# Layout of the prepared second-layer weights in DRAM, the pair job's places and one product's turn in a three-stage network on one Trainium2 core

## The chip, the core and the metric

The kernel runs on one core of a Trainium2 chip. The metric is the time of one launch in device microseconds (us). Five instruction streams run side by side: TensorE (PE, matmuls; its weight loads are PEld), VectorE (DVE), ScalarE (ACT), GpSimd (POOL) and SyncE (SP). Here SP issues all DMAs; its queue is shown as SPq. Each engine works through its own list in order and waits at semaphores for the others.

## What is computed

Attention with a window and a few global tokens gives 2176 rows of 512. Two networks follow, one a mixture of eight experts, one plain:

```python
x = attn_out.transpose(0, 2, 1, 3).reshape(2176, 512)
P = exp(x @ w_gate - max)                       # then 8 rounds of scaling rows and columns
for e in range(8):                              # w1: 512 x 1024, w2: 1024 x 512 per expert
    out += P[:, e:e+1] * (np.maximum(x @ w1[e], 0) @ w2[e])
h = out @ w_in                                  # 512 x 2048
y = np.where(h > 0, h, np.exp(np.minimum(h, 0)) - 1) @ w_out
```

All is float32. TensorE takes its operands as a rounded high part (names with h) and the remainder as a low part (l), so a product is three matmuls: high by high, high by low and low by high.

## The kernel before

**Products.** The large products are made by the seven-product method for 2 by 2 blocks: sums and differences of blocks of the weights (`t1` to `t4`) and of the activations (`s1` to `s4`) are prepared, seven products are taken, and their results are added up. Blocks that need no sum are called by row and column: `11`, `12`, `21`, `22`. "Prepared weights" are those sums and blocks, each as a high and a low part.

**Stages.** Up to about 240 us: attention and the first units. From 240 to about 860 us, the **first pass**: fourteen units (half an expert each) over the first 1024 tokens, by `mix_0`, layer one on lines L1383 to L1385 into banks `q`, layer two on L158 to L162. Beside its products a unit prepares the weights of the next one and stores them in DRAM, as the second pass needs them again: `pw1` for the expert's layer one (`store1`), `pw2` for its layer two (`weights2`, with `store` for the sums and `store_raw` for the plain blocks). From 860 to about 1600 us, the **second pass**: the other tokens, sixteen units of two halves each (g=0 with 256 columns, g=1 with 320), by `mix_1`; `load2` brings the prepared weights of layer two back. From 1600 us: the **last network**, whose layer one loads its prepared `w_in` from `wq` by `layer_one` (7 names, high and low, 14 loads of 128 KB at each of 14 calls, 196 in all).

**Jobs beside the units.** The weights of the last network are prepared in pieces beside the units. A **pair** (`weights64_pair`) takes two chunks of `w_in`, builds one unit's seven operands and stores them to `wq`; units 2, 4 and 6 of the first pass hold one each, and units 23, 24, 25, 27 and 28 (the second pass begins with 14) the other five. Other jobs are `prepare` (units 15, 17, 19, 21), `back` (16, 18, 20, 22), which turns finished rows over, and in the first pass `xr` sums (units 3, 5, 7, 9), whose loads stand among the next unit's.

**What sets the order.** SP's queue takes DMAs in the order in which the program gives them. In the first pass the steps of a unit go to two lists that `mix_0` works off, `side1` and `side2`. `lds`, the job's loads, stand at the end of `side2`. In the second pass the steps of a job are put at places of a unit given by `SPOTS`; places below 22 lie in g=0, the others in g=1. The products of a half are ordered by `MIX_1`: `a` and `b` are the two chains of layer one (128 columns of the prepared weights each), `t` the products of layer two, `p` and `tx` those left over from before. In that list the number is the product.

**Which banks.** In `Fold`, products 1, 6, 7 and 4 of a chain add up in one bank, `f1` (`BANK`). After products 1, 6 and 7 ScalarE copies the bank out (`s1`, `u2`, `u3`, by `KEEP`, line L1392) and only then may the chain's next product write it. After `a7` VectorE adds `u3` to a stored part (`t`, L798), and ScalarE makes `v22` of it (L1530). After `t1` ScalarE copies its bank to `f2` (L1629), the seed that t6 adds to. The next operand's high part `hs4` is a ScalarE cast (L1543).

**Stores of a pair before** (L1094): for each of high and low part, seven DMAs, each of two pieces of 128 numbers (512 bytes) for a partition.

```python
for i, v in enumerate((t[:, 0], t[:, 1], t[:, 2], p1[:, 256:], p0[:, :256], p1[:, :256], t[:, 3])):
    nc.sync.dma_start(wq[q][:, u, i, :, k], v.rearrange("p (f c) -> p f c", f=2))
```

The raw blocks of `pw2` (L945) go in four DMAs for each part, each of two pieces of 256 numbers (1 KB) for a partition.

Of the kernel before, what the change touches and what calls it, by code (L numbers as in the profile page):

```python
# [11 lines left out]
F32 = mybir.dt.float32  # L12
# [39 lines left out]
    "pair": (4, 6, 7, 9, 10, 12, 13, 15, 17, 19, 20, 21, 22, 23, 25),  # L52
# [8 lines left out]
MIX_1 = "a1 b1 p4 a2 b2 p3 a6 b6 a5 b5 a7 b7 t1 a4 b4 a3 t6 b3 t2 t5 t7 tx"  # L61
# [8 lines left out]
WORDER = ("t1", "t3", "t4", "22", "11", "21", "t2")  # L70
XORDER = ("11", "12", "21", "22", "s1", "s2", "s3", "s4")
XUSE = ("11", "12", "s2", "s1", "s3", "22", "s4")
W2ORDER = ("11", "t2", "21", "22", "t1", "t3", "t4")
# [12 lines left out]
def tile_net(ctx: ExitStack, tc, kq, vw, vc, qg, wg, w1, w2, wi, wo, consts, out):  # L86
    nc = tc.nc
    U1 = 2 * E
    U2 = F2 // FU
# [18 lines left out]
    wq = {p: dram.tile([128, U2, 7, 2, 2, 128], F32, tag="wq" + p, name="wq" + p) for p in "hl"}  # L108
    pw1 = {p: dram.tile([128, U1, 7 * 512], F32, tag="pw1" + p, name="pw1" + p) for p in "hl"}
    pw2 = {p: dram.tile([128, U1, 8, 512], F32, tag="pw2" + p, name="pw2" + p) for p in "hl"}  # L110
# [802 lines left out]

    def weights2(u):
        v = {}
# [21 lines left out]
        def store(n):  # L937
            for q, t in (("h", v[n, "h"].bitcast(F32)), ("l", v[n, "l"])):
                nc.sync.dma_start(pw2[q][:, u, W2ORDER.index(n)], t)

        def store_raw(q):
            for n in ("11", "12", "21", "22"):
                i, j = int(n[0]) - 1, int(n[1]) - 1
                o = pw2[q][:, u, 7 if n == "12" else W2ORDER.index(n)]
                nc.sync.dma_start(  # L945
                    o.rearrange("p (k f) -> p k f", k=2), w2s[q][:, 2 * i:2 * i + 2, 256 * j:256 * j + 256].bitcast(F32)
                )
# [25 lines left out]
    def prepare(second, u):  # L973

        src, dst, order = ((w1, pw1, WORDER), (w2, pw2, W2ORDER + ("12",)))[second]
# [17 lines left out]
        def lo(n):  # L993
            comb(blk(n).bitcast(F32R), blk(n), v[n, "h"].bitcast(F32), ALU.subtract)
            i = order.index(n)
            for q, t in (("h", v[n, "h"].bitcast(F32)), ("l", blk(n))):
                o = dst[q][:, u, i * 512:(i + 1) * 512] if not second else dst[q][:, u, i]
                nc.sync.dma_start(o.rearrange("p (k f) -> p k f", k=2), t)
# [67 lines left out]
    def weights64_pair(u, k):  # L1066
# [24 lines left out]
        def store():  # L1091
            for q, t, p1, p0 in (("h", c1.room(F32, 4), c1.p, c0.p), ("l", c0.room(F32, 4), c1.t, c0.t)):
                for i, v in enumerate((t[:, 0], t[:, 1], t[:, 2], p1[:, 256:], p0[:, :256], p1[:, :256], t[:, 3])):
                    nc.sync.dma_start(wq[q][:, u, i, :, k], v.rearrange("p (f c) -> p f c", f=2))  # L1094
# [71 lines left out]
    def layer_one(u, f, names=WORDER):  # L1166
        for n in names:
            for q in "hl":
                nc.sync.dma_start(
                    wop[n + q][:, :, f * 128:f * 128 + 128].bitcast(F32), wq[q][:, u, WORDER.index(n), f]  # L1170
                )
# [500 lines left out]
    def load2(u, names):  # L1672
        for n in names:
            for q in "hl":
                i = W2ORDER.index(n) if n != "12" else 7
                o = W2ORDER.index(n if n != "12" else "t2")
                nc.sync.dma_start(fold["all" + q][:, o * 512:(o + 1) * 512].bitcast(F32), pw2[q][:, u, i])
# [25 lines left out]
    with tc.manual_schedule():  # L1703
# [89 lines left out]
        for a, u in enumerate(range(2, U1)):  # L1793
# [11 lines left out]
            if build1:  # L1805
                side2.extend(mingle(build2, steps + build1[:8]))
                loads2, casts, build2 = weights2(u + 1)
                side2.extend(loads2 + build1[8:] + lds)
            else:
                side2.extend([lambda: second_x(XUSE, GS[1][0], SL)] + mingle(build2, steps))  # L1810
# [234 lines left out]
```

## Time and profile before

| | us |
|---|---|
| median of 3 runs | 2014.83 (2011.32 to 2018.03) |
| the profiled execution | 2016.9 |
| its span | 2015.1 |
| TensorE busy | 1899.3 (94% of the span) |
| VectorE busy | 1416.9 (70%) |
| ScalarE busy | 987.3 (49%) |
| DMA engines, mean share of the span | 67.6% |

All rows come from the one profiled execution; times are counted from the start of its span. A row of the timeline gives the start, the length, the engine, the line, the operation, what it writes and from what, shapes, and a count where several alike follow one another. A bracket at its end tells how long the engine was idle before it and what it was waiting for. The rows of stretches give, for a window, its length, each engine's busy time with its instructions, the granted clock of TensorE as a share of full speed (1.00 is 2.4 GHz, 0.50 is 1.2 GHz), the busy share of the 16 DMA engines, and the rate. That share can come out a little above 1.00.

### The profile page before, as it was taken

Reading aid. Unit: us, or ns where it says so; the run is one execution under the profiler, and the core shown is the slowest. Engines: PE = TensorE matmul, PEld = TensorE weight load, DVE = VectorE, ACT = ScalarE, POOL = GpSimd, SP = SyncE. Lnnn points to the kernel's source line nnn. Section 1 sums busy time; section 2 is a strip of 40 time slices with the busy share of each in tenths; the row PEclk is TensorE's granted clock in tenths of the full one; section 3 lists DMA queues with packets and bytes.
Section 4 is the critical chain, followed back from the end, with each engine's and each line's share of the span. In section 5 each row is a group of like instructions: output and inputs, shape, how many; then the busy total and the mean of one; then the engine's idle time right before and its main releaser. Section 6 shows DMA issues by size and latency. Waiting matters only on the chain.

```text
span 2015.1 us, 35891 instructions
## 1 busy us (share of the span) xinstructions
PE 1899.3 (94%) x13345; PEld 1677.7 (83%) x13345; DVE 1416.9 (70%) x2783; ACT 987.3 (49%) x2125; POOL 272.5 (14%) x294
## 2 busy tenths in 40 slices
PE   8999999798989999999999999898989999999999
PEld 6877777676767787799999999888988987788998
DVE  4554877575767568657767777777677578888887
ACT  5453443343434334356555555455555554555664
POOL 2135222222222222100000000000000000002322
PEclk9999999898989999999999999999999999999999
DMA  7585776767677767887786878555655796654431
GB/s 248 195 282 173 270 268 236 272 233 278 234 286 293 276 234 284 269 301 267 244 285 235 292 248 288 176 191 201 220 189 184 246 300 193 189 201 155 121 116 68
DMA packets 338638, 465.52 MB, mean 231 GB/s; under 512 B 35104, under 2 KB 212768, under 8 KB 335136
## 3 DMA queue, kind: packets, MB, share of 16 engines
q1 hardware_dynamic: 338464, 463.24, 67.6%
q8 instruction: 105, 1.72, 0.3%
q14 instruction: 69, 0.57, 0.1%
HBM read 282.12 MB, written 181.01 MB: 230 GB/s over the span
## 4 chain that ended last, share of the span: by engine, by line
PE 49%; DVE 14%; DMA 6%; ACT 4%; issue 2%; SPq 2%; POOL 0%; DVEq 0%; ACTq 0%; POOLq 0%
PE m L162 4%; PE f L1383 4%; PE m L160 4%; PE m L158 4%; PE f L1385 4%; PE f L1384 4%; PE f L1621 4%; PE f L1623 4%; PE f L1622 4%; PE q L1322 2%; PE q L1321 2%; PE q L1320 2%; DVE acc L1458 2%; PE q L1383 2%; PE q L1384 2%
## 5 line engine op out<-in xcount | busy, mean ns | idle before, releaser
L162 PE MATMUL m<-w2h,hl 128*128 128x512 f32 x784 | 309.9, 395 | 4.9 <-DVE hl L1284 3.4
L158 PE MATMUL m<-w2h,hh 128*128 128x512 f32 x784 | 309.1, 394 | 5.7 <-DVE aside L1913 3.0
L160 PE MATMUL m<-w2l,hh 128*128 128x512 f32 x784 | 309.4, 395 | 3.1 <-POOL w2l L154 3.1
L1284 POOL TENSOR_TENSOR hl<-eg,hh 128x288 fp32r<-128x288 f32 (+1 forms) x80 | 57.0, 722 | 1114.2 <-DMA xs4h<-xo3h 983.7
L162 PEld LDWEIGHTS m<-w2h,hl 128*128 128x128 f32 x784 | 147.9, 189 | 39.6 <-DVE hl L1284 6.7
L158 PEld LDWEIGHTS m<-w2h,hh 128*128 128x128 f32 x784 | 148.1, 189 | 35.7 <-DVE aside L1913 3.3
L160 PEld LDWEIGHTS m<-w2l,hh 128*128 128x128 f32 x784 | 148.1, 189 | 33.9 <-POOL w2l L154 5.2
L1621 PE MATMUL f<-wfh,hs 128*128 128x256 f32 x512 | 149.2, 291 | 3.1 <-ACT f L1629 3.1
L1623 PE MATMUL f<-wfh,ls 128*128 128x256 f32 x512 | 148.1, 289 | 0.0
L1622 PE MATMUL f<-wfl,hs 128*128 128x256 f32 x512 | 148.1, 289 | 0.0
L1621 PE MATMUL f<-wfh,h 128*128 128x256 f32 x384 | 109.4, 285 | 2.1 <-ACT u L1633 2.1
L1421 ACT ACTIVATE hh<-t 128x512 fp32r<-128x512 f32 x64 | 40.6, 635 | 142.8 <-DVE t L798 142.5
L1622 PE MATMUL f<-wfl,h 128*128 128x256 f32 x384 | 108.8, 283 | 0.2 <-DMA wfl<-pw2l 0.2
L1623 PE MATMUL f<-wfh,l 128*128 128x256 f32 x384 | 108.8, 283 | 0.0
L154 POOL TENSOR_TENSOR w2l<-w2r,w2h 128x512 fp32r<-128x512 f32 x56 | 73.2, 1335 | 256.8 <-ACT w2h L150 190.7
L1458 DVE SCALAR_TENSOR_TENSOR acc<-y,pr,acc 128x512 f32<-128x512 f32 x120 | 84.9, 749 | 30.2 <-ACT y L1650 28.4
L1621 PEld LDWEIGHTS f<-wfh,hs 128*128 128x128 f32 x512 | 101.2, 198 | 4.8 <-ACT f L1629 4.4
L1392 ACT COPY u<-f 128x256 f32<-128x256 f32 (+1 forms) x128 | 50.5, 400 | 106.1 <-PE f L1385 103.9
L1623 PEld LDWEIGHTS f<-wfh,ls 128*128 128x128 f32 x512 | 101.5, 198 | 0.0
L1622 PEld LDWEIGHTS f<-wfl,hs 128*128 128x128 f32 x512 | 101.4, 198 | 0.0
L798 DVE TENSOR_TENSOR t<-f,u 128x256 f32<-128x256 f32 (+1 forms) x128 | 58.2, 455 | 60.1 <-ACT u L1392 39.5
L798 DVE TENSOR_TENSOR t<-q,u 128x512 f32<-128x512 f32 x56 | 38.6, 689 | 83.2 <-PE q L1385 49.5
(405 smaller groups left out, 5743.9 us busy)
## 6 DMA issues: line engine op xcount, KB each, us to landing
wfh<-pw2h SPq DMA_DIRECT2D x128, 256.0 KB, 4.5
wfl<-pw2l SPq DMA_DIRECT2D x128, 256.0 KB, 4.9
wh<-pw1h SPq DMA_DIRECT2D x105, 256.0 KB, 5.3
wl<-pw1l SPq DMA_DIRECT2D x105, 256.0 KB, 5.3
pw1h<-wh SPq DMA_DIRECT2D x13, 1792.0 KB, 11.9
pw1l<-wl SPq DMA_DIRECT2D x13, 1792.0 KB, 15.5
wr<-in_w_dram SPq DMA_DIRECT2D x36, 512.0 KB, 7.6
w2r<-in_w_dram SPq DMA_DIRECT2D x28, 512.0 KB, 5.8
```

Of the source, the lines that this page charges most:

```text
L154: e.tensor_tensor(out=lo, in0=src, in1=hi.bitcast(F32), op=ALU.subtract)
L158: nc.tensor.matmul(ps, ah, bh, start=first, stop=False)
L160: nc.tensor.matmul(ps, ah, bl, start=False, stop=False)
L162: nc.tensor.matmul(ps, al, bh, start=False, stop=last)
L798: nc.vector.tensor_tensor(out=o, in0=a, in1=b, op=op)
L1383: nc.tensor.matmul(ps, wh, xh, start=k == 0 and begin, stop=False, skip_group_check=True)
L1384: nc.tensor.matmul(ps, wh, xl, start=False, stop=False, skip_group_check=True)
L1385: nc.tensor.matmul(ps, wl, xh, start=False, stop=k == 1, skip_group_check=True)
L1458: nc.vector.scalar_tensor_tensor(out=acc, in0=y, scalar=scale, in1=acc, op0=ALU.mult, op1=ALU.add)
L1621: nc.tensor.matmul(ps[:, m], hh, wh, start=begin and m == k == 0, stop=False, skip_group_check=True)
L1622: nc.tensor.matmul(ps[:, m], hh, wl, start=False, stop=False, skip_group_check=True)
L1623: nc.tensor.matmul(ps[:, m], hl, wh, start=False, stop=m == k == 1, skip_group_check=True)
```

## The change

1. `wq` has a layout in which a pair's operands lie behind one another: the pair's store is three DMAs for each part (four operands of 4 KB for a partition, two of 2 KB, one of 1 KB) in place of seven. `layer_one` reads two pieces of 512 bytes for a partition in place of one of 1 KB.
2. `pw2` is split. The sums stay in it; the plain blocks go to `pr2`, whose layout is that of the tile in SBUF, so that `store_raw` is one DMA of 1 MB (8 KB for a partition) in place of four. `load2` reads a plain block as two pieces of 1 KB.
3. In `side2` the job's loads `lds` stand ahead of the last build steps.
4. The places of "pair" are moved back: eight of its steps stay in g=0, where there were twelve; the other seven are in g=1.
5. In `MIX_1` t1 stands between a7 and b7.

```diff
--- before.py
+++ after.py
@@ -49,7 +49,7 @@
 PAIRS = (2, 4, 6, 23, 24, 25, 27, 28)
 SPOTS = {
     "single": (26, 28, 30, 31, 33, 35),
-    "pair": (4, 6, 7, 9, 10, 12, 13, 15, 17, 19, 20, 21, 22, 23, 25),
+    "pair": (8, 10, 12, 13, 15, 16, 18, 20, 22, 24, 27, 29, 31, 33, 34),
     "prepare": (7, 8, 9, 10, 14, 15, 18, 19, 20, 23, 24, 27, 29, 30, 33, 34, 36, 37, 40, 41),
 }
 SEEDED = 6
@@ -58,7 +58,7 @@
 GS = ((0, 256), (256, HALF))
 MIX_0 = "01 05 02 06 11 07 12 04 16 03 15 17"
 MIX_F = "a1 a5 b1 b5 a2 b2 a6 b6 a7 b7 a4 b4 a3 b3"
-MIX_1 = "a1 b1 p4 a2 b2 p3 a6 b6 a5 b5 a7 b7 t1 a4 b4 a3 t6 b3 t2 t5 t7 tx"
+MIX_1 = "a1 b1 p4 a2 b2 p3 a6 b6 a5 b5 a7 t1 b7 a4 b4 a3 t6 b3 t2 t5 t7 tx"
 MIX_L = "a1 b1 p4 a2 b2 p3 a6 b6 a5 b5 a7 b7 t1 a4 b4 a3 b3 t2 t6 t5 t7"
 MIX_E = "p4 t1 p3 t2 t6 t5 t7 t4 t3 tx"
 KEEP = {1: "s1", 6: "u2", 7: "u3"}
@@ -70,6 +70,7 @@
 WORDER = ("t1", "t3", "t4", "22", "11", "21", "t2")
 XORDER = ("11", "12", "21", "22", "s1", "s2", "s3", "s4")
 XUSE = ("11", "12", "s2", "s1", "s3", "22", "s4")
+QORDER = ("t1", "t3", "t4", "t2", "21", "22", "11")
 W2ORDER = ("11", "t2", "21", "22", "t1", "t3", "t4")
 W22 = ("11", "t2", "21", "t3", "t1", "t4", "22")
 TURN_0 = "a1 a6 a2 a7 a5 a4"
@@ -105,9 +106,10 @@
     sf = {p: dram.tile([128, 4, 2, SL], F32, tag="sf" + p, name="sf" + p) for p in "hl"}
     yd = dram.tile([128, TP[0] // 128, D], F32, tag="yd", name="yd")
     wd = {p: dram.tile([128, U2, 4, 512], F32, tag="wd" + p, name="wd" + p) for p in "hl"}
-    wq = {p: dram.tile([128, U2, 7, 2, 2, 128], F32, tag="wq" + p, name="wq" + p) for p in "hl"}
+    wq = {p: dram.tile([128, U2, 2, 7, 256], F32, tag="wq" + p, name="wq" + p) for p in "hl"}
     pw1 = {p: dram.tile([128, U1, 7 * 512], F32, tag="pw1" + p, name="pw1" + p) for p in "hl"}
-    pw2 = {p: dram.tile([128, U1, 8, 512], F32, tag="pw2" + p, name="pw2" + p) for p in "hl"}
+    pw2 = {p: dram.tile([128, U1, 4, 512], F32, tag="pw2" + p, name="pw2" + p) for p in "hl"}
+    pr2 = {p: dram.tile([128, U1, 4, 512], F32, tag="pr2" + p, name="pr2" + p) for p in "hl"}
     xo = {
         (p, q): dram.tile([128, 16, TP[p - 2] // 2], F32, tag=f"xo{p}{q}", name=f"xo{p}{q}") for p in (2, 3) for q in "hl"
     }
@@ -911,6 +913,12 @@
                 i = WORDER.index(n)
                 nc.sync.dma_start(wall[q][:, i * 512:(i + 1) * 512].bitcast(F32), pw1[q][:, u, i * 512:(i + 1) * 512])
 
+    def block2(q, u, n):
+        if n[0] == "t":
+            return pw2[q][:, u, int(n[1]) - 1].rearrange("p (k f) -> p k f", k=2)
+        i, j = int(n[0]) - 1, int(n[1]) - 1
+        return pr2[q][:, u, 2 * i:2 * i + 2, 256 * j:256 * j + 256]
+
     def weights2(u):
         v = {}
 
@@ -936,15 +944,10 @@
 
         def store(n):
             for q, t in (("h", v[n, "h"].bitcast(F32)), ("l", v[n, "l"])):
-                nc.sync.dma_start(pw2[q][:, u, W2ORDER.index(n)], t)
+                nc.sync.dma_start(block2(q, u, n), t.rearrange("p (k f) -> p k f", k=2))
 
         def store_raw(q):
-            for n in ("11", "12", "21", "22"):
-                i, j = int(n[0]) - 1, int(n[1]) - 1
-                o = pw2[q][:, u, 7 if n == "12" else W2ORDER.index(n)]
-                nc.sync.dma_start(
-                    o.rearrange("p (k f) -> p k f", k=2), w2s[q][:, 2 * i:2 * i + 2, 256 * j:256 * j + 256].bitcast(F32)
-                )
+            nc.sync.dma_start(pr2[q][:, u], w2s[q].bitcast(F32))
 
         def cast(k):
             split(w2s["h"][:, k], w2s["l"][:, k], v[k // 2][:, k % 2])
@@ -972,7 +975,7 @@
 
     def prepare(second, u):
 
-        src, dst, order = ((w1, pw1, WORDER), (w2, pw2, W2ORDER + ("12",)))[second]
+        src, order = ((w1, WORDER), (w2, W2ORDER + ("12",)))[second]
         v, names = {}, [n for n in order if n[0] != "t"]
 
         def load(i):
@@ -994,8 +997,8 @@
             comb(blk(n).bitcast(F32R), blk(n), v[n, "h"].bitcast(F32), ALU.subtract)
             i = order.index(n)
             for q, t in (("h", v[n, "h"].bitcast(F32)), ("l", blk(n))):
-                o = dst[q][:, u, i * 512:(i + 1) * 512] if not second else dst[q][:, u, i]
-                nc.sync.dma_start(o.rearrange("p (k f) -> p k f", k=2), t)
+                o = block2(q, u, n) if second else pw1[q][:, u, i * 512:(i + 1) * 512].rearrange("p (k f) -> p k f", k=2)
+                nc.sync.dma_start(o, t)
 
         d = [("d", "t1", "12", "11"), ("d", "t2", "22", "t1"), ("d", "t4", "21", "t2"), ("d", "t3", "22", "12")]
         steps = [d[0], d[1], "ht1", "lt1", "h11", "l11", d[2], "ht2", "lt2", "ht4", "lt4", d[3], "ht3", "lt3"]
@@ -1090,8 +1093,9 @@
 
         def store():
             for q, t, p1, p0 in (("h", c1.room(F32, 4), c1.p, c0.p), ("l", c0.room(F32, 4), c1.t, c0.t)):
-                for i, v in enumerate((t[:, 0], t[:, 1], t[:, 2], p1[:, 256:], p0[:, :256], p1[:, :256], t[:, 3])):
-                    nc.sync.dma_start(wq[q][:, u, i, :, k], v.rearrange("p (f c) -> p f c", f=2))
+                nc.sync.dma_start(wq[q][:, u, k, 0:4], t)
+                nc.sync.dma_start(wq[q][:, u, k, 4:6], p1.rearrange("p (j f) -> p j f", j=2))
+                nc.sync.dma_start(wq[q][:, u, k, 6], p0[:, :256])
 
         return [c0.load, c1.load], [
             c0.words, c0.sign, c0.rest, c1.words, c0.value, c1.sign, c1.rest, c1.value,
@@ -1167,7 +1171,7 @@
         for n in names:
             for q in "hl":
                 nc.sync.dma_start(
-                    wop[n + q][:, :, f * 128:f * 128 + 128].bitcast(F32), wq[q][:, u, WORDER.index(n), f]
+                    wop[n + q][:, :, f * 128:f * 128 + 128].bitcast(F32), wq[q][:, u, :, QORDER.index(n), f * 128:f * 128 + 128]
                 )
 
     def layer_two(u, f):
@@ -1672,9 +1676,9 @@
     def load2(u, names):
         for n in names:
             for q in "hl":
-                i = W2ORDER.index(n) if n != "12" else 7
                 o = W2ORDER.index(n if n != "12" else "t2")
-                nc.sync.dma_start(fold["all" + q][:, o * 512:(o + 1) * 512].bitcast(F32), pw2[q][:, u, i])
+                to = fold["all" + q][:, o * 512:(o + 1) * 512].bitcast(F32)
+                nc.sync.dma_start(to.rearrange("p (k f) -> p k f", k=2), block2(q, u, n))
 
     def mix_1(order, quads, tails, at, items, rush=False):
 
@@ -1805,7 +1809,7 @@
             if build1:
                 side2.extend(mingle(build2, steps + build1[:8]))
                 loads2, casts, build2 = weights2(u + 1)
-                side2.extend(loads2 + build1[8:] + lds)
+                side2.extend(loads2 + build1[8:13] + lds + build1[13:])
             else:
                 side2.extend([lambda: second_x(XUSE, GS[1][0], SL)] + mingle(build2, steps))
             mix_0(u, at)
```

**SP in the first pass, the unit after a pair unit**, from the pair's stores to the next loads; `w2r` is the next unit's layer-two weights. Before:

```order
L1094 DMA wqh<-r_4329 128x2x128 x3
L1094 DMA wqh<-cp 128x2x128 x3
L1094 DMA wqh<-r_4329 128x2x128
L1094 DMA wql<-r_4327 128x2x128 x3
L1094 DMA wql<-ct 128x2x128 x3
L1094 DMA wql<-r_4327 128x2x128
L939 DMA pw2h<-w2ht_4612 128x512
L939 DMA pw2l<-w2t_4570 128x512
L939 DMA pw2h<-w2ht_4631 128x512
L939 DMA pw2l<-w2t_4604 128x512
L945 DMA pw2l<-w2l 128x2x256 x4
L919 DMA w2r<-in_w_dram 128x1024 x2
```

and now:

```order
L1096 DMA wqh<-r_4307 128x1024
L1097 DMA wqh<-cp 128x512
L1098 DMA wqh<-cp 128x256
L1096 DMA wql<-r_4301 128x1024
L1097 DMA wql<-ct 128x512
L1098 DMA wql<-ct 128x256
L947 DMA pw2h<-w2ht_4591 128x512
L947 DMA pw2l<-w2t_4557 128x512
L947 DMA pw2h<-w2ht_4610 128x512
L947 DMA pw2l<-w2t_4583 128x512
L950 DMA pr2l<-w2l 128x2048
L927 DMA w2r<-in_w_dram 128x1024 x2
```

The 14 stores of `wq` are 6 and the 4 raw ones are 1; nothing changes places, and `lds` (the `xr` loads that follow `w2r`) stand where they stood.

**ScalarE in the second pass, first half of a unit without a job**, from the copies after a7 and b7 on; `u3` is the copy out of a chain's bank (`f1`, here one number for chain a and one for chain b), `v22` what is made of VectorE's `t`, `f2` the seed from t1. Before:

```order
L1392 COPY u3_15795<-f1_15669 128x256
L1392 COPY u3_15806<-f1_15678 128x256
L1530 ACTIVATE v22_15810<-t_15797 128x256
L1629 COPY f2_15825<-f1_15812 128x512
L1530 ACTIVATE v22_15810<-t_15808 128x256
L1543 CAST hs4_15828<-os4_15708 128x512
L1530 ACTIVATE v21_15846<-f1_15669 128x256
L1530 ACTIVATE v21_15846<-f1_15678 128x256
```

and now:

```order
L1396 COPY u3_15665<-f1_15539 128x256
L1633 COPY f2_15683<-f1_15670 128x512
L1534 ACTIVATE v22_15685<-t_15667 128x256
L1547 CAST hs4_15687<-os4_15578 128x512
L1396 COPY u3_15695<-f1_15548 128x256
L1534 ACTIVATE v22_15685<-t_15697 128x256
L1534 ACTIVATE v21_15716<-f1_15539 128x256
```

The copy after b7 (`u3` of the second `f1`) stood second; now it stands behind the seed, the first `v22` and `hs4`.

## Rows read from the trace of the kernel before

**Rows 1.** The page's first part: engine, busy us, share of the span, instructions.

```profile
PE 1899.3 (94%) x13345; PEld 1677.7 (83%) x13345; DVE 1416.9 (70%) x2783; ACT 987.3 (49%) x2125; POOL 272.5 (14%) x294
```

**Rows 2.** TensorE's waits, 340 to 860 us: engine, line, releaser, us in total, times, longest.

```profile
PE q L1383 <- DVE t L798: 23.8, 7, 9.2
PE q L1383 <- ACT u L1392: 15.3, 2, 11.8
PE q L1383 <- ACT q L1389: 4.6, 5, 1.0
```

**Rows 3.** The timeline of SP's queue: start, length, line, operation, out<-in, count.

```profile
340.75 1.51 SPq L1094 DMA_DIRECT2D wqh<-r  x3
350.50 2.74 SPq L945 DMA_DIRECT2D pw2l<-w2l  x4
```

**Rows 4.** Stretches: length, PE, PEld, DVE, ACT, POOL, granted clock, DMA share, GB/s.

```profile
340.75:348.40 7.65, 7.65 (x35) 6.31 (x34) 7.65 (x12) 3.84 (x8) 1.29 (x1) 1.00 0.83 243
348.40:353.30 4.90, 4.90 (x23) 4.01 (x23) 3.11 (x5) 1.10 (x3) 0.00 (x0) 1.00 0.99 340
353.30:363.04 9.74, 1.46 (x7) 0.88 (x5) 0.00 (x0) 0.00 (x0) 0.00 (x0) 0.83 1.04 331
364.00:368.00 4.00, 1.43 (x3) 1.16 (x4) 3.77 (x9) 2.31 (x5) 0.00 (x0) 0.50 1.06 448
439.12:462.71 23.59, 17.01 (x74) 13.40 (x72) 10.77 (x16) 6.58 (x12) 1.28 (x1) 0.99 0.92 285
537.69:560.57 22.88, 17.02 (x74) 13.40 (x72) 10.77 (x16) 6.59 (x12) 1.28 (x1) 0.94 0.96 307
```

**Rows 5.** The timeline around the three long stalls; brackets: idle before, and its releaser.

```profile
363.07 1.23 DVE L798 TENSOR_TENSOR xr<-xr 128x1024 f32<-128x1024 f32 x1 [11.55 <-DMA xr<-xdl]
366.57 0.80 PE L1383 MATMUL q<-x22h,wh 128*128 128x512 f32 x1 [11.82 <-ACT u L1392]
...
466.36 0.79 PE L1383 MATMUL q<-xs4h,wh 128*128 128x512 f32 x1 [9.21 <-DVE t L798]
...
564.25 0.80 PE L1383 MATMUL q<-xs4h,wh 128*128 128x512 f32 x1 [8.54 <-DVE t L798]
```

**Rows 6.** TensorE's waits, 860 to 1600 us: the columns of rows 2.

```profile
PE f L1383 <- DVE t L798: 16.2, 5, 3.2
PE f L1383 <- ACT f L1389: 8.6, 6, 2.0
PE f L1621 <- ACT f L1629: 3.1, 4, 0.8
```

**Rows 7.** Timeline of two first halves: with a prepare job, and with none.

```profile
993.79 0.28 PE L1383 MATMUL f<-xs3h,wh 128*128 128x256 f32 x1
...
997.92 0.42 ACT L1530 ACTIVATE v<-t 128x256 f32<-128x256 f32 x1 [1.58 <-DVE t L798]
...
1436.05 0.28 PE L1383 MATMUL f<-xs3h,wh 128*128 128x256 f32 x1
...
1437.49 0.28 PE L1621 MATMUL f<-wfh,h 128*128 128x256 f32 x1
...
1437.75 0.37 ACT L1392 COPY u<-f 128x256 f32<-128x256 f32 x1 [0.40 <-PE f L1385]
...
1439.17 0.57 ACT L1629 COPY f<-f 128x512 f32<-128x512 f32 x1 [0.38 <-PE f L1623]
...
1439.97 0.61 ACT L1543 CAST hs<-os 128x512 fp32r<-128x512 f32 x1
```

**Rows 8.** Second half of a pair unit: timeline, then a stretch (columns of rows 4).

```profile
1294.29 1.05 ACT L1085 CAST r<-r 128x1024 fp32r<-128x1024 f32 x1
...
1300.82 0.42 PE L1383 MATMUL f<-x12h,wh 128*128 128x320 f32 x1 [1.82 <-ACT f L1389]
...
1301.80:1305.20 3.40, 3.40 (x18) 3.40 (x17) 2.15 (x4) 0.44 (x1) 0.00 (x0) 0.50 1.08 370
```

**Rows 9.** A stretch at the start of the last stage, columns of rows 4.

```profile
1600.00:1625.00 25.00, 24.08 (x176) 23.47 (x175) 12.66 (x22) 11.95 (x27) 0.00 (x0) 1.00 1.08 363
```


## The prediction

> **What bounds the kernel now.** TensorE is busy for 94% of the span [rows 1], so the time moves only where TensorE waits, or where a wait of its own is made. I read in this order: the list of TensorE's waits by stage, then the timeline around the longest, then SP's queue and the DMA share in the same stretch, then ScalarE's order around the places where the new table puts instructions.
>
> In the first pass (to about 860 us) TensorE's waits for layer one's products are 23.8 + 15.3 + 4.6 = 43.7 us in 14 stalls [rows 2], and three of them, 11.8, 9.2 and 8.5 us, make 29.5 [rows 5]. All three are alike: VectorE idles 11.55 us for `xr<-xdl`, a DMA, and TensorE goes on 3.5 us after it [rows 5]. The DMA is late because it stands at the end of a queue: SP issues the 14 stores of `wq` (from 340.75 on), the stores of layer two's weights (the raw ones at 350.50), `w2r`, then `xr`, without a gap [rows 3]. The DMA engines are 0.83 busy while `wq` is stored and 0.99 to 1.04 from there on [rows 4]. So both the issuing and the engines' work count, the first only in the first third.
>
> In the second pass (860 to 1600) the waits are shorter and belong to VectorE and ScalarE: 16.2 us for `t`, 8.6 for `f`, 3.1 for the seed of `t1` at t6 [rows 6].
>
> **The change, part by part.**
>
> *Fewer and longer stores.* 14 stores of `wq` become 6, and 4 raw ones become 1, with the same bytes (1.84 and 1.05 MB). What the engines gain from longer pieces I bound by rates. The stretch with the 512-byte pieces moved 243 GB/s at a share of 0.83, 293 at full share; the stretch of 2 KB pieces and raw ones 340 at 0.99, 343; the stretch with the very long pieces of `pw1` 448 at 1.06, 423 [rows 4]. 1.84 MB take 6.3 us at 293, 5.4 at 343 and 4.3 at 423. The new pieces are 4, 2 and 1 KB, between these; I take 4.6, nearer to the long end since four sevenths of the bytes go in the longest. Gain 1.7 us. The raw 1.05 MB go from 3.06 us (at 343) to 2.48 (at 423), gain 0.6. The engines' idle share goes as well, as the queue no longer lags: against the 1.04 of a stretch that only waits for DMAs, 0.83 over 7.65 us and 0.99 over 4.90 leave 1.8 us; the other two stretches, 0.92 of 23.59 and 0.96 of 22.88, leave 2.7 and 1.7 [rows 4]. Each stall shrinks by 2.3 plus its idle part: 4.1 + 4.9 + 4.0, in sum **-13.0 us**. Ends: idle against a share of 1.00 alone, 1.3 + 1.9 + 0.9 = 4.1; and the queue's issue time as the sole limit: 6 issues for 14 at a third of 1.51 each (3.0 for 7.65) and one for four (0.7 for 2.74) [rows 3], 6.7 each, 20. What is late next stays the same wait, some 8, 4 and 4 us long, so the half clock after it (0.50 at 364 to 368 [rows 4]) stays too.
>
> Units without a pair store have the raw part of it: 1.05 MB right ahead of the next loads. The other 11 stalls hold 14.2 us [rows 2, 5]; 0.6 each gives **-6.6 us**. Ends: 0, if a stall ends on something else, and 11, if all of 0.7 against 2.74 counts.
>
> *The list `side2`.* `lds` now stands ahead of the last build steps. Those steps issue no DMA, and the order shows SP's queue as before, so the loads do not stand further forward by this. Only a VectorE subtraction changes place with its neighbour. I take 0.
>
> *"pair" later in SPOTS.* In the second pass a pair's sums, casts, subtractions and store leave the first half (g=0) for the second, and the ScalarE casts stand behind the chain that frees TensorE there: one alone is 1.05 us [rows 8], and two smaller ones and the four sums on VectorE leave the way to `f` too. TensorE's wait in such a second half is 1.82 us [rows 8]; five of the six in the group, 7.6 of 8.6 us, are of this kind [rows 6]. They go, and with two of them 3.4 us at half clock (0.50 [rows 8]), 1.7 us lost each: **-11.0 us**. Ends: 0 (something on VectorE is late next) and -14.3. In the first halves VectorE's `t` of a7 comes earlier, by the two steps that go behind it, and a3's 3.2 us five times [rows 6] would go. They come back one product earlier, at b4 (below); I take **0**.
>
> *MIX_1: t1 between a7 and b7.* On ScalarE `u3` of b7 now stands behind the seed of t1, the `v22` of a7 and an `hs4`. b4 accumulates into the bank that this copy empties, so it waits for all three. The half at 1436: a7 begins at 1436.05, twelve matmuls later t1 at 1437.49 [rows 7], so 0.12 each; a product is six (0.72), t1 twelve (1.44). New: t1 is done 0.72 earlier, the seed begins at 1438.45 (1439.17 less 0.72), then `v22`, and `hs4` at 1439.25 (seed to `hs4` is 0.80); `u3` of b7 begins at 1439.76 (`hs4` takes 0.61, and ScalarE's rows overlap by a tenth) and is done by 1440.18 (0.37 and a step to TensorE) [rows 7]. b4 is due at 1436.05 + 0.72 + 1.44 + 0.72 + 0.72 = 1439.65. TensorE waits 0.5 us where it waited for nothing. By the same steps, with each half's own times: two clean first halves 1.0; 15 second halves, whose products are longer, 0.3 each, 4.4; four first halves with a prepare job 7.3, since VectorE's `t` there lets `v22` start only at 997.92, with a7 begun at 993.79: `hs4` 998.24, `u3` 998.75, b4 999.17 for 997.39 [rows 7], 1.75 us; four with a back job 1.2 each, 4.8; five pair halves, where a step of the pair's stands on ScalarE ahead of `u3` as well, 3.3 for the 3.2 at a3, 0.3. Sum **+17.8 us**. On the other side the seed comes earlier, and t6's wait of 3.1 us [rows 6] goes: **-3.1 us**. The 1.75 us waits lie near the size at which the clock fell (a wait of 1.82 was followed by 0.50 [rows 8]); I count one such dip, **+1.7 us**. Ends of this part: -3.1 (`u3` is never late) and +37 (rival 1).
>
> *Loads with shorter pieces.* Layer one now loads `wq` in 512-byte pieces: 128 KB at 293 instead of 343 GB/s is 0.06 us more of the engines' time, 196 times, and the half of layer two's loads that come from `pr2` likewise. The one stretch where the engines have no room is the start of the last stage (share 1.08, TensorE 24.08 of 25 us busy [rows 9]), with some 28 such loads: between 0 and 1.8 us. I take **+1.0 us**.
>
> **Sum.** -13.0 - 6.6 - 11.0 - 3.1 + 17.8 + 1.7 + 1.0 = -13.2 us. The profiled execution would go from 2016.9 (span 2015.1) to 2003.7; it lies 2 us above the median of 2014.83, and against the median I say **2001.6 us**.
>
> A rule speaks against the largest term. The Trainium skill, page "DMA: Bandwidth & Descriptors", section Specifications, gives 512 B as the least transfer at line rate; by it the 512-byte pieces of `wq` lose nothing. The rows say 293 against 343 to 423 GB/s, so I go by them; what the rule gives is rival 2.
>
> **The rivals.**
>
> 1. *The b4 wait takes the clock with it: slower.* In 13 first halves (prepare, back, pair) TensorE then waits 1.2 to 3.5 us at b4. If each is followed by 3.4 us at half clock, 22 us are lost, 20.4 more than I count: 2022.0. For it: 1.82 us sufficed once [rows 8], and the pair halves have it already. Against it: most of the waits are under that. [...]
>
> 2. *The engines gain nothing from longer pieces.* Only the idle shares go, 4.1 of the 13.0 us (against a share of 1.00), and the 6.6 shrink to half: 2001.6 + 8.9 + 3.3 = 2013.8, no change that can be told. For it: the share from 348.40 on is at 0.99 to 1.04 [rows 4], so the engines are the limit there. Against it: the rates in the same rows.
>
> 3. *The queue is the limit.* 20 us instead of 13.0, and 11 instead of 6.6: 1990.2. For it: the issues follow each other without a gap, and the share is 0.83 beneath them. Against it: the shares after it.
>
> 4. *`u3` is not late*, because ScalarE's three steps fit under a4 after all or TensorE makes the loss good at a wait that follows. 19.5 us less: 1982.1. For it: in the clean half it is a matter of 0.5 us, and each half has later waits that could absorb some. Against: the order on ScalarE is fixed and each step has a measured duration.
>
> That the loads do not move forward by the list is counted at 0 above and alters none of these.
>
> **How the numbers follow.** Forecast 0.50 (1994 to 2009 by itself), rival 1 0.08, rival 2 0.12, rival 3 0.17, rival 4 0.13. A measurement here tells about 0.3%, 6 us, from no change. Faster by more: rivals 3 and 4, nine tenths of the forecast, in sum 0.75. Within: the rest of the forecast and most of rival 2, 0.16. Slower: rival 1 and an end of rival 2, 0.09. The range, with rival 4's centre and the upper side of rival 1 left out, is 1984 to 2015.
>
> **What would show it.** Right: the three stalls near 366, 466 and 564 us at about 8, 4 and 4 us, with the `wq` stores over in about 4.8 us; no wait for `f` in the second halves of pair units; no wait at t6; new waits of L1387 (b4) for ScalarE's `u`, 0.3 to 0.5 us in most halves and 1.2 to 3.5 in 13. Wrong: if the three stalls keep their length, if the second halves wait for VectorE instead, or if b4 waits nowhere, or more than 25 us in all.

## The result and the profile after

The changed kernel takes 1997.87 us (median of 4 runs, 1995.0 to 1998.6) against 2016.43 for the kernel before (4 runs beside it, 2011.32 to 2019.58). The ratio is 0.9908, interval 0.9884 to 0.9932: faster by 0.7 to 1.2%. The forecast was 2001.6 us.

The profiled executions differ by more than the change explains, so I split them at the same instructions of TensorE's list (its 3400th, 5990th and 11300th of 13345, the same products in all kernels here): ahead of the first pass, first pass, second pass, last network. The times run from TensorE's first product to its last.

| us | ahead | first pass | second pass | last network |
|---|---|---|---|---|
| before | 217.2 | 656.4 | 740.4 | 395.6 |
| after | 212.3 | 641.6 | 741.6 | 394.4 |
| difference | -4.9 | -14.7 | +1.2 | -1.2 |
| forecast | 0 | -19.6 | +5.4 | +1.0 |

The first column has nothing of the change in it: the first store that the change touches is issued at 226.6 us before and at 224.8 after, and the column lies between 212.3 and 218.6 in all fourteen profiles of this study, whatever the kernel. What is left, -14.7 us, is near the sum of -13.2; but it was made of two errors of 4 to 5 us that cancel, and that is luck. The medians differ by 18.6 us, with an interval of 13.7 to 23.4; the 14.7 lies in it, the forecast's 13.2 just below.

TensorE's waits in the first pass after the change, 340 to 860 us (engine, line, releaser, us in total, times, longest), which answer to [rows 2]:

```profile
PE q L1387 <- DVE t L800: 13.3, 5, 5.5
PE q L1387 <- ACT u L1396: 11.8, 2, 8.6
PE q L1387 <- ACT q L1393: 4.6, 5, 1.0
```

43.7 us became 29.7. The second pass, 860 to 1600 us, which answers to [rows 6]:

```profile
PE f L1387 <- ACT u L1396: 28.6, 25, 3.1
PE f L160 <- DMA wfh<-pr2h: 0.9, 1, 0.9
PE f L1387 <- ACT f L1393: 0.9, 1, 0.9
```

The waits for VectorE's `t` and for t6's seed are gone, those for `f` are down to one, and 25 new ones of 28.6 us stand at ScalarE's `u`, the copy out of a chain's bank.

SP's queue in the unit after the first pair unit (start, length), answering to [rows 3], then the stretches of this unit and three of the second pass (columns of rows 4):

```profile
334.44 0.47 SPq L1096 DMA_DIRECT2D wqh<-r  x1
334.97 0.44 SPq L1097 DMA_DIRECT2D wqh<-cp  x1
335.46 1.16 SPq L1098 DMA_DIRECT2D wqh<-cp  x1
...
341.59 0.59 SPq L950 DMA_DIRECT2D pr2l<-w2l  x1
342.23 1.93 SPq L927 DMA_DIRECT2D w2r<-in_w_dram  x2
```

```profile
334.44:339.18 4.74, 4.74 (x22) 3.92 (x21) 4.74 (x8) 2.66 (x5) 0.00 (x0) 1.00 0.93 359
339.18:342.20 3.02, 3.02 (x15) 2.47 (x14) 3.02 (x5) 1.26 (x4) 1.30 (x1) 1.00 1.02 371
342.20:353.53 11.33, 6.28 (x28) 4.85 (x26) 3.03 (x6) 1.00 (x2) 0.00 (x0) 0.96 1.04 352
981.40:984.80 3.40, 3.37 (x28) 3.37 (x29) 3.35 (x7) 2.21 (x6) 0.00 (x0) 1.00 0.31 96
1271.80:1275.20 3.40, 3.40 (x16) 3.40 (x17) 3.33 (x7) 1.58 (x4) 0.00 (x0) 0.50 0.00 0
1323.60:1327.00 3.40, 3.35 (x28) 3.35 (x29) 3.31 (x7) 1.68 (x5) 0.00 (x0) 1.00 0.00 0
```

The `wq` stores occupy SP from 334.44 to 339.18, 4.74 us where it had been 7.65. The rate there is 359 GB/s at a share of 0.93, which makes 386 at full share, where the stretch with the 512-byte pieces makes 293 [rows 4]. The three long stalls (answering to [rows 5]):

```profile
353.53 1.23 DVE L800 TENSOR_TENSOR xr<-xr 128x1024 f32<-128x1024 f32 x1 [8.30 <-DMA xr<-xdl]
357.03 0.80 PE L1387 MATMUL q<-x22h,wh 128*128 128x512 f32 x1 [8.56 <-ACT u L1396]
...
452.53 0.80 PE L1387 MATMUL q<-xs4h,wh 128*128 128x512 f32 x1 [5.04 <-DVE t L800]
...
546.35 0.80 PE L1387 MATMUL q<-xs4h,wh 128*128 128x512 f32 x1 [5.53 <-DVE t L800]
```

They are 8.6, 5.0 and 5.5 us, 10.4 less than before.

### The profile page after: what moved, and what is told of

It reads as the page before. It is cut to its first block, busy times and chain, and to the rows that moved or that the text cites. A ratio compares the mean times of both kernels' runs of the same rounds, so it can differ in the third digit from the quotient of the medians.

```text
span 1995.8 us, 35647 instructions
## 1 busy us (share of the span) xinstructions
PE 1895.4 (95%) x13345; PEld 1671.2 (84%) x13345; DVE 1416.3 (71%) x2783; ACT 987.9 (49%) x2125; POOL 273.4 (14%) x294
## 4 chain that ended last, share of the span: by engine, by line
PE 63%; DVE 17%; DMA 7%; ACT 6%; issue 3%; SPq 2%; POOL 1%; DVEq 0%; ACTq 0%; POOLq 0%
PE m L164 6%; PE m L160 6%; PE m L162 6%; PE f L1627 4%; PE f L1387 4%; PE f L1625 4%; PE f L1626 4%; PE f L1389 4%; PE f L1388 4%; DVE acc L1462 3%; PE q L1387 3%; PE q L1389 2%; PE q L1388 2%; PE q L1326 2%; PE q L1325 2%
## 5 line engine op out<-in xcount | busy, mean ns | idle before, releaser
L160 PE MATMUL m<-w2h,hh 128*128 128x512 f32 x784 | 308.8, 394 | 5.6 <-DVE aside L1917 3.0
L160 PEld LDWEIGHTS m<-w2h,hh 128*128 128x128 f32 x784 | 147.9, 189 | 35.5 <-DVE aside L1917 3.3
## 6 DMA issues: line engine op xcount, KB each, us to landing
pw1l<-wl SPq DMA_DIRECT2D x13, 1792.0 KB, 16.3
```

What stands on the lines that cost most here:

```text
L160: nc.tensor.matmul(ps, ah, bh, start=first, stop=False)
```

## The experiments

All times are medians; a ratio, with its interval, is to the kernel before on the same chip, and can differ a little from the quotient of the medians. The stage columns come from one profile each, split as above. Five kernels with the second pass in the old order (before, and experiments 1, 5, 6 and 10) lie between 737.1 and 740.4 us in it, and five with the first pass of the changed kernel (after, 1, 3, 7 and 9) between 639.0 and 641.6; so differences of about 3 us in these columns tell nothing.

| kernel | us | ratio (95%) | first pass | second pass |
|---|---|---|---|---|
| stores alone | 2001.43 | 0.9922 (0.9897 to 0.9947) | 640.2 | 739.9 |
| order alone | 2015.29 | 0.9998 (0.9981 to 1.0015) | 657.1 | 738.4 |
| changed, old MIX_1 | 1974.30 | 0.9789 (0.9765 to 0.9812) | 639.0 | 713.9 |
| new MIX_1 alone | 2029.25 | 1.0061 (1.0041 to 1.0082) | 657.2 | 753.2 |
| `wq` alone | 2009.12 | 0.9980 (0.9960 to 1.0000) | 652.6 | 737.1 |
| raw blocks alone | 2009.76 | 0.9974 (0.9957 to 0.9992) | 651.4 | 740.2 |
| changed, old MIX_1, t6 late | 1984.07 | 0.9855 (0.9831 to 0.9879) | 640.4 | 727.9 |
| changed, old MIX_1, job's loads first | 1945.93 | 0.9671 (0.9656 to 0.9687) | 614.4 | 715.6 |
| changed, `lds` back | 1999.23 | 0.9917 (0.9886 to 0.9948) | 639.6 | 740.8 |
| before, job's loads first | 1989.09 | 0.9868 (0.9833 to 0.9903) | 628.9 | 738.3 |
| job's loads ahead of the raw store too | 1940.19 | 0.9622 (0.9597 to 0.9648) | 606.3 | 716.6 |
| and ahead of the last sums | 1933.79 | 0.9586 (0.9572 to 0.9600) | 600.4 | 716.0 |

**1. The two layouts without the new order.** The changed kernel with three edits taken back:

```diff
-    "pair": (8, 10, 12, 13, 15, 16, 18, 20, 22, 24, 27, 29, 31, 33, 34),
+    "pair": (4, 6, 7, 9, 10, 12, 13, 15, 17, 19, 20, 21, 22, 23, 25),
-MIX_1 = "... a7 t1 b7 a4 ..."
+MIX_1 = "... a7 b7 t1 a4 ..."
-                side2.extend(loads2 + build1[8:13] + lds + build1[13:])
+                side2.extend(loads2 + build1[8:] + lds)
```

> The kernel before with the two new layouts alone (wq and pr2); SPOTS, MIX_1 and side2 as before. Theory: the whole gain of the first pass comes from here. The three long stalls fall from 11.8, 9.2, 8.5 us to about 8.6, 5.0, 5.5 as in the changed kernel, the first pass ends about 15 us earlier, the second pass is as before (waits of 16.2 us for t, 8.6 for f, 3.1 at t6). Time: before minus 15 us, ratio 0.992 to 0.993. Rival: the gain is due to the order of the steps and the loads; then under 5 us, ratio over 0.997.

Measured: ratio 0.9922, first pass 16.2 us shorter, second pass 0.5. Its waits, from 240 to 865 us (where the changed kernel has 16.4, 13.3 and 4.6) and from 865 to 1620:

```profile
PE q L1387 <- ACT u L1396: 16.7, 4, 8.8
PE q L1387 <- DVE t L800: 13.1, 5, 5.6
...
PE f L1387 <- DVE t L800: 16.2, 5, 3.2
PE f L1387 <- ACT f L1393: 8.3, 5, 2.4
PE f L1625 <- ACT f L1633: 3.1, 4, 0.8
```

The layouts carry the gain of the first pass, as the theory had it; the second pass keeps the waits of [rows 6].

**2. The new order without the layouts.**

```diff
-MIX_1 = "... a7 b7 t1 a4 ..."
+MIX_1 = "... a7 t1 b7 a4 ..."
-    "pair": (4, 6, 7, 9, 10, 12, 13, 15, 17, 19, 20, 21, 22, 23, 25),
+    "pair": (8, 10, 12, 13, 15, 16, 18, 20, 22, 24, 27, 29, 31, 33, 34),
```

> The kernel before with the new SPOTS and the new MIX_1, old layouts. Theory: the second pass gets its new waits at b4 (28.6 us in the changed kernel) and loses 16.2 (a3), 7 (f) and 3.1 us (t6) and two or three stretches at half clock, which comes out at 0 to +2 us; first pass as before. Ratio 1.000 to 1.001. Rival: the order edits bring a gain of their own of 5 us or more.

Measured: ratio 0.9998, no change; the second pass is 738.4 us long for 740.4, which is within the spread. The two edits together are worth nothing, and the next two runs tell them apart.

**3. The changed kernel with t1 back behind b7.**

```diff
-MIX_1 = "... a5 b5 a7 t1 b7 a4 b4 a3 t6 b3 ..."
+MIX_1 = "... a5 b5 a7 b7 t1 a4 b4 a3 t6 b3 ..."
```

> The changed kernel with MIX_1 as before (a7 b7 t1). Theory: the waits of 28.6 us at b4 are the price of t1 standing between a7 and b7. They go; t6's 3.1 us come back, and a3 waits about 0.7 us in five pair halves. Time: 22 us below the changed kernel, about 1976 us, ratio to before about 0.980. Rival: TensorE makes the loss good elsewhere, or VectorE's t at a3 is late next by the old 3.2 us; then within 10 us of the changed kernel, 1988 us or more.

Measured: 1974.30 us, 23.6 below the changed kernel's 1997.87. Its waits from 865 to 1620 us:

```profile
PE f L1625 <- ACT f L1633: 5.7, 9, 0.8
PE f L1387 <- ACT f L1393: 4.8, 5, 1.0
PE f L1387 <- DVE t L800: 3.3, 5, 0.7
```

All 28.6 us at `u` are gone; t6's seed costs 5.7 us, where 3.1 were expected, and a3's `t` 3.3 us in five halves, 0.7 each at most, as expected. So t1's new turn alone costs more than the whole change gains. The run shows another thing beside: it differs from the kernel of experiment 1 by SPOTS (and by `lds`, which does nothing, experiment 9), and its second pass is 713.9 us long where that one's is 739.9. So SPOTS alone is worth 26 us with the old MIX_1: 12.9 of a3's 16.2, 3.5 of the waits for `f`, and over 10 us of TensorE's time outside of its waits (708.3 us against 697.7). The granted clock goes with it: 0.98 over the second pass of experiment 1, 1.00 here, where no half-clock stretch follows a wait. What t1's new turn costs is plain in a first half without a job; these are ScalarE's rows in the changed kernel and then TensorE's first matmul of b4 (answering to [rows 7]):

```profile
1419.88 0.37 ACT L1396 COPY u<-f 128x256 f32<-128x256 f32 x1 [1.06 <-PE f L1389]
1421.37 0.57 ACT L1633 COPY f<-f 128x512 f32<-128x512 f32 x1 [1.11 <-PE f L1627]
1421.85 0.42 ACT L1534 ACTIVATE v<-t 128x256 f32<-128x256 f32 x1
1422.17 0.61 ACT L1547 CAST hs<-os 128x512 fp32r<-128x512 f32 x1
1422.67 0.38 ACT L1396 COPY u<-f 128x256 f32<-128x256 f32 x1
...
1423.10 0.39 PE L1387 MATMUL f<-x22h,wh 128*128 128x256 f32 x1 [0.39 <-ACT u L1396]
```

The copy after b7 stands behind the seed (1421.37), `v` and `hs`; b4 waits 0.39 us for it. In the first half of a pair unit a step of the pair (`r<-r`) stands there too, and everything behind `v`, which waits for VectorE:

```profile
1270.02 0.42 ACT L1534 ACTIVATE v<-t 128x256 f32<-128x256 f32 x1 [2.13 <-DVE t L800]
1270.34 0.60 ACT L1547 CAST hs<-os 128x512 fp32r<-128x512 f32 x1
1270.85 0.65 ACT L1044 ACTIVATE r<-r 128x512 f32<-128x512 uint32 x1
1271.40 0.35 ACT L1396 COPY u<-f 128x256 f32<-128x256 f32 x1
...
1271.80 0.58 PE L1387 MATMUL f<-x22h,wh 128*128 128x256 f32 x1 [3.14 <-ACT u L1396]
```

**4. New MIX_1 alone.**

```diff
-MIX_1 = "... a7 b7 t1 a4 ..."
+MIX_1 = "... a7 t1 b7 a4 ..."
```

> The kernel before with the new MIX_1 alone. Theory: b4 waits in all halves; in the five first halves of pair units for longer than in the changed kernel, since VectorE's t is 2.6 us later there (5.7 us each in place of a3's 3.2). 41 us of new waits less 16.2 and 3.1 us that go: about 22 us slower than before, ratio about 1.011. Rival: no change, within 6 us.

Measured: ratio 1.0061, 13 us slower, the second pass 12.8 us longer. Its waits from 865 to 1620 us:

```profile
PE f L1383 <- ACT u L1392: 39.0, 25, 5.4
PE f L1383 <- ACT f L1389: 2.1, 2, 1.9
```

39.0 us of new waits, 5.4 the longest, close to the expected 41 and 5.7. But those for `f` fell from 8.6 to 2.1, which the expectation had left as they were; that the delay at b4 gives ScalarE the time that it lacked later in a pair unit fits this, but no run shows it by itself. So a third of the loss is made good, and the price was overstated by 9 us. The two edits do not add up: SPOTS alone is worth 26 us, t1's turn costs 12.8 alone, and both together change nothing (experiment 2). With the new SPOTS the same turn costs 24.5 to 27.7 us (738.4 and 741.6 against 713.9), for with the old ones it took a3's 16.2 us away, of which the new ones take 12.9 away without it.

**5 and 6. The layouts one by one.**

```diff
-    wq = {p: dram.tile([128, U2, 7, 2, 2, 128], F32, tag="wq" + p, name="wq" + p) for p in "hl"}
+    wq = {p: dram.tile([128, U2, 2, 7, 256], F32, tag="wq" + p, name="wq" + p) for p in "hl"}
...
+                nc.sync.dma_start(wq[q][:, u, k, 0:4], t)
+                nc.sync.dma_start(wq[q][:, u, k, 4:6], p1.rearrange("p (j f) -> p j f", j=2))
+                nc.sync.dma_start(wq[q][:, u, k, 6], p0[:, :256])
```

> The kernel before with the new layout of wq alone. Both new layouts together shortened the first pass by 15 to 16 us. Theory: wq's part is the issue gaps (1.8 us a stall) and the longer pieces (1.7), 2.5 to 3.5 us in each of the three long stalls and nothing in other units: first pass 8 to 10 us shorter. Rival: the raw stores carry most of it, wq under 4 us.

```diff
+    pr2 = {p: dram.tile([128, U1, 4, 512], F32, tag="pr2" + p, name="pr2" + p) for p in "hl"}
...
         def store_raw(q):
+            nc.sync.dma_start(pr2[q][:, u], w2s[q].bitcast(F32))
```

> The kernel before with the raw blocks in pr2 alone, wq as before. Theory: about 0.6 us in each unit whose loads stand behind the raw store: 0.5 to 1 us in each of the three long stalls and 0.2 to 0.8 us in the shorter ones, 5 to 7 us in all. Rival: nothing in the shorter ones, 2 us in all.

Measured: medians 6.1 and 5.5 us below the kernel before; by the ratios 4 and 5 us, the first with an interval that ends at 1.0000. The profiles tell the parts apart: with `wq` alone the three long stalls are 10.1, 6.2 and 5.4 us, 7.9 less:

```profile
363.51 0.80 PE L1385 MATMUL q<-x22h,wh 128*128 128x512 f32 x1 [10.08 <-ACT u L1394]
...
460.57 0.79 PE L1385 MATMUL q<-xs4h,wh 128*128 128x512 f32 x1 [6.16 <-DVE t L799]
...
554.12 0.80 PE L1385 MATMUL q<-xs4h,wh 128*128 128x512 f32 x1 [5.43 <-DVE t L799]
```

(L1385 is L1383 of the kernel before.) With the raw blocks alone they are 11.9, 8.8 and 8.2, 0.6 less, while the shorter waits from 340 us on fall by about 4. So `wq` serves the long stalls and the raw blocks the short ones, though the raw blocks were also expected to take 0.5 to 1 us from each long stall. The two first passes are 3.8 and 5.0 us shorter, both together 16.2. For `wq` alone 8 to 10 were expected and a rival named under 4: the gain at the stalls came, that of the whole pass did not. With `wq` alone some short waits in units that hold no pair store are longer than before (643: 2.56 for 2.28, 683: 3.94 for 3.53, 776: 1.22 for 0.39 us), and with either layout alone the two waits at the end of the pass take 4.6 and 4.0 us for 2.9. No run here says why, and it stays open.

**7. t6 behind b3.** The changed kernel with the old place of t1 and

```diff
-MIX_1 = "... a7 b7 t1 a4 b4 a3 t6 b3 t2 ..."
+MIX_1 = "... a7 b7 t1 a4 b4 a3 b3 t6 t2 ..."
```

> The changed kernel with the old place of t1 and with t6 behind b3 (a7 b7 t1 a4 b4 a3 b3 t6). With the old place of t1 t6 waits 5.7 us in nine halves for ScalarE's seed. Theory: b3 covers it (0.7 us in a first half), and nothing else waits for t6: 5 us below the kernel with the old MIX_1, about 1969 us. Rival: what follows t6 (the DMA behind it, the copy of its bank) comes later and tx or the next half waits for it: no gain, 1974 us or more.

Measured: 1984.07 us, 9.8 above the kernel of experiment 3; the rival held. Its waits from 860 to 1620 us:

```profile
PE f L160 <- DMA wfh<-pr2h: 10.0, 5, 2.9
PE f L1387 <- ACT f L1393: 7.0, 5, 1.6
```

t6 waits no more, but the load that takes the place of t6's operands is issued after t6, and the products that need it (L160, tx) wait 10.0 us in five halves, up to 2.9. Three of the five are followed by a stretch at a granted clock of 0.50, and TensorE's time outside of its waits in this pass is 705.7 us for 697.7.

**8. The job's loads really further forward.** The changed kernel with the old MIX_1 and

```diff
-                side2.extend(loads2 + build1[8:13] + lds + build1[13:])
+                side2.extend(lds + loads2 + build1[8:])
```

> The changed kernel with the old MIX_1, and with lds ahead of loads2 in side2, so that a job's loads really stand further forward in SP's queue, ahead of w2r's two loads of 512 KB. Theory: what VectorE waits for in the first pass is the job's load and w2r's 1.05 MB in front of it; it lands 2.5 us earlier (1.05 MB at 423 GB/s). The three long stalls fall by 2.5 us each, the shorter ones of units with xr loads by up to theirs: 7 to 14 us less than the kernel with the old MIX_1, 1960 to 1967 us. Rival: w2r is needed just as soon, and VectorE or GpSimd waits for it instead: within 3 us of that kernel.

Measured: 1945.93 us, 28.4 below the kernel of experiment 3 and twice what was expected. SP's queue and VectorE's wait in the same unit:

```profile
334.63 0.59 SPq L1096 DMA_DIRECT2D wqh<-r  x1
...
341.56 0.55 SPq L950 DMA_DIRECT2D pr2l<-w2l  x1
342.16 2.02 SPq L819 DMA_DIRECT2D xr<-xdh  x2
344.22 2.18 SPq L819 DMA_DIRECT2D xr<-xdl  x2
346.45 0.99 SPq L927 DMA_DIRECT2D w2r<-in_w_dram  x2
...
350.95 1.22 DVE L800 TENSOR_TENSOR xr<-xr 128x1024 f32<-128x1024 f32 x1 [5.55 <-DMA xr<-xdl]
354.46 0.79 PE L1387 MATMUL q<-x22h,wh 128*128 128x512 f32 x1 [5.82 <-ACT u L1396]
```

From the first `wq` store (334.63) to `xr` in place (350.95) it takes 16.3 us, against 19.1 in the changed kernel (334.44 to 353.53): w2r's 1.05 MB is out of the way, 2.8 us. The long stalls are 5.8, 2.0 and 1.5 us. The waits of the first pass for layer one's products fall from 33.5 to 15.7 us. The rest of the 24.6 us by which the first pass is shorter than in experiment 3 comes without waits: TensorE's time outside of them falls from 597.2 to 589.7 us, since the stretches at half clock that follow the stalls are fewer (granted clock of the first pass 0.97 and 0.99). That part the expectation had left out.

**9. `lds` back at the end of `side2`.** The changed kernel with

```diff
-                side2.extend(loads2 + build1[8:13] + lds + build1[13:])
+                side2.extend(loads2 + build1[8:] + lds)
```

> The changed kernel with lds at the end of side2 again, as before. Theory: SP's queue has the same order either way, so the edit does nothing: within 4 us of the changed kernel, about 1998 us, and the waits of the first pass the same within 0.5 us each. Rival: the loads do gain by it; then the three long stalls are 1 us or more longer each than in the changed kernel.

Measured: 1999.23 us; first pass 639.6 for 641.6; the long stalls 8.4, 4.7 and 5.5 us for 8.6, 5.0 and 5.5. The edit does nothing, as SP's queue, unchanged by it, had told.

**10. The job's loads first, nothing else.** The kernel before with

```diff
-                side2.extend(loads2 + build1[8:] + lds)
+                side2.extend(lds + loads2 + build1[8:])
```

> The kernel before with nothing changed but lds ahead of loads2 in side2, so that the job's loads stand ahead of w2r's in SP's queue. Theory: as much as with the new layouts (21 to 28 us there), since it takes w2r's 1.05 MB out of the way in every unit; the three long stalls fall by 2.5 to 4 us each. About 1992 us, ratio 0.987 to 0.990. Rival: with the old layouts the queue is so late that the loads gain less than 8 us, ratio over 0.996.

Measured: 1989.09 us, ratio 0.9868, the first pass 27.5 us shorter: by the medians this one line brings more than the whole change (28.8 us for 18.6), though the intervals of the two ratios overlap at their ends. The long stalls are 9.3, 6.0 and 5.1 us, 2.5 to 3.4 less each, as expected.

**11 and 12. Further forward.** As experiment 8, but with the loads put into the list ahead of its last steps; `m` is the list of steps and stores:

```diff
-                side2.extend(mingle(build2, steps + build1[:8]))
+                m = mingle(build2, steps + build1[:8])
                 loads2, casts, build2 = weights2(u + 1)
-                side2.extend(lds + loads2 + build1[8:])
+                side2.extend(m[:-3] + lds + m[-3:] + loads2 + build1[8:])
```

> The kernel with the old MIX_1 and lds ahead of loads2, with lds moved once more, ahead of the store of the raw low part (1.05 MB). Theory: the wait of VectorE is set by what stands in SP's queue ahead of the job's load, byte by byte; the three stalls of 5.8, 2.0 and 1.5 us lose up to 2.5 us each and the two short ones of 0.9 and 0.7 go, 6 to 8 us in all: 1938 to 1940 us. Rival: the raw store is then late, its tile w2l comes free late, and GpSimd and layer two wait for it: no gain, 1944 us or more.

Experiment 12 has 6 in place of 3, which puts two stores of sums behind the loads as well.

> As the kernel before it, with lds ahead of the last two stores of sums (0.5 MB) too. Theory: another 1.2 us at the one stall that is left, within 2 us of the kernel with lds ahead of the raw store. Rival: the loads' buffer is not free yet, so that they hold up the stores behind them: slower than that kernel by 3 us or more.

Measured: 1940.19 and 1933.79 us. The first was expected at 1938 to 1940, but not by the right parts: the short stalls went, and the one at 355 us, the longest, lost 0.7 us and not 2.5 (5.8 to 5.1). The second was expected within 2 us of the first and is 6.4 lower: there the same stall falls to 1.8 us. Together the two moves gave what the bytes say (1.05 and 0.5 MB for 4.0 us); why the megabyte gave less than the half behind it stays open. Neither rival shows: GpSimd's `w2l` costs layer two 2.7 us, as it did with 2.8 in experiment 8. Waits of the last one from 240 to 865 us:

```profile
PE q L1387 <- ACT q L1393: 4.5, 5, 1.0
PE m L162 <- POOL w2l L156: 2.7, 4, 1.3
PE q L1387 <- ACT u L1396: 2.0, 2, 1.8
PE q L1387 <- DVE t L800: 0.2, 1, 0.2
```

It is the fastest kernel of this study, 0.9586 of the kernel before (0.9572 to 0.9600), against 0.9908 for the change.

## Why the prediction was right

The time, the sign and the mechanisms came as forecast; the sizes did not all, and the first and the second pass were off by +4.9 and -4.2 us. Step by step:

- **Three long stalls**, forecast -13.0 us, measured -10.4. The rate was right: 1.84 MB in 4.6 us was the estimate, 386 GB/s make it 4.75. The term of idle engines was too large: I took the whole lag of the queue as gained. From the first `wq` store to `xr` in place the stretch shrank from 22.3 to 19.1 us, 3.2 and not 4.1. The stores now leave SP sooner, but the loads behind them took 11.3 us from SP's first issue (342.2) where they had taken 9.8, and the engines moved 3.99 MB in that time for 3.22 (rate times length), stores that were still to be moved. By share times length the engines worked 21.3 us in the old stretch and 19.3 in the new: some 2 us of the 3.2 come from the pieces, near the 2.3 forecast, and about 1.2 from idle time, where 1.8 was forecast. Experiments 5 and 6 show that `wq` carries this term.
- **The other stalls**, forecast -6.6, measured -3.6: the 11 others from 340 us on went from 14.2 us to 10.6, in 9 stalls. With two stalls between 240 and 340 us that the forecast had left out it is -5.0 (49.7 to 34.3 us in all, less the 10.4). The 0.6 us of each was too much, as five of the 11 wait for ScalarE at L1389 and kept their 4.6 us [rows 2].
- **`lds`**, forecast 0, measured 0 (experiment 9).
- **Second halves of pair units**, forecast -11.0: the waits for `f` there went from 7.6 to 0.9 us, -6.7, and after that one the clock stays at 1.00; with the two half-clock stretches of 1.7 us it is -10.1.
- **First halves of pair units**, forecast 0: b4 waits 3.14 us in each where a3 waited 3.24. The forecast held to 0.1.
- **b4**, forecast +17.8 net of a3's, measured 28.6 less 16.2, +12.4. Prepare halves 1.2 to 1.6 us (forecast 1.75), back halves 1.1 (1.2), clean ones 0.39 (0.5). The term that was off most is that of the second halves, about 1.7 us in all for 4.4: there TensorE's products are longer and ScalarE's steps fit under a4 for the most part. Rival 4 was true of this one kind of half. The forecast named more than 25 us at b4 as a sign of being wrong, and 28.6 is more; but its own terms, with 3.3 us for each pair half, come to 1.0 + 4.4 + 7.3 + 4.8 + 16.5 = 34.0 before a3's waits are taken off, so that the sign contradicted the sum, and the waits came out under the sum.
- **t6**, forecast -3.1, and it went.
- **The clock**, forecast +1.7 for the waits near 1.75 us: after none of the eight waits of 1.08 to 1.63 us in prepare and back halves did the clock fall (981 to 985 at 1.00), so rival 1 fell. The five pair halves had the lower clock before; four keep it (1271.8 at 0.50) and one does not (1323.6 at 1.00).
- **Shorter pieces of loads**, forecast +1.0, measured nothing that one profile could show: the last network is 1.2 us shorter, and the second pass waits for the `pr2` loads as long as it did for `pw2`'s, 1.9 us.

The second pass by these terms is -10.1 + 12.4 - 3.1 = -0.8 us; it measured +1.2, and the difference is within the spread of this column.

Rival 2, that longer pieces gain nothing, fell with the rate of 386 for 293 GB/s. The Trainium skill, page "DMA: Bandwidth & Descriptors", section Specifications, puts the least transfer at line rate at 512 B; by that the 512-byte stores of `wq` had nothing to gain. The trace disagrees: 293 is a quarter less than 386. Rival 3, the queue as the sole limit, fell too: with six issues for fourteen some took longer, up to 1.16 us for 0.5, at shares of 0.93 to 1.04.

What the forecast did not ask was whether t1's new turn was worth having. Its own terms had the answer: without that edit its price (17.8) and its dip of the clock (1.7) go, t6's 3.1 us come back, and a3's 16.2, which the new SPOTS take away and the forecast let come back at b4, are gained: 2001.6 - 17.8 - 1.7 + 3.1 - 16.2 = 1969.0 us. The run without it took 1974.3 (experiment 3).

## What to carry to other kernels

When an engine waits for a load, write down what stands ahead of that load in its queue and count the bytes: here one megabyte taken out of the way was worth 2.6 to 4.0 us of each long stall (experiment 8). The bytes are a guide and no rule: another megabyte was worth 0.7 us to the longest (experiment 11). Moving the load ahead of work that nobody waits for brought more here than making that work cheaper (28.8 us by the medians in experiment 10, 14.4 in experiment 1). A move in a program's list changes a queue only if something that the queue issues lies in between; look at the queue's own order first. Before a product is given an earlier turn, list what the engine that empties its bank has to do ahead of the copy that the next product needs.

## What the runs showed of the hardware

- A stretch of mostly 512-byte stores moved 243 GB/s at a DMA share of 0.83, one of stores in pieces of 4, 2 and 1 KB 359 at 0.93; that makes 293 and 386 at full share.
- SP's time for one DMA was no constant here and did not go by its size: the old 128 KB stores of `wq` took 0.5 us each; of the new ones the 512 KB took 0.47 us, the 128 KB 1.16, and the raw store of 1 MB 0.59.
- TensorE's time outside of its waits differs between kernels with the same work: 597 us in the first pass with stalls of 8 us, 590 and 586 with stalls of 6 and 2. Of the 20 waits of 3 us or more between 240 and 1600 us in the kernels before and after, 19 were followed by work at a granted clock of 0.50; these stretches are 3.4 to 10.2 us long, part of it still in the wait.
